# Sliding-window attention in front of an MLP: 64 queries against 128 keys in six of eight batches, instead of 128 keys against 192 queries

## The chip, the cores and the metric

The kernel runs on one core of one Trainium2 chip, in one launch. The metric is the device time in microseconds (us) of that core; less is better. The time before is the median of 13 runs, 317.54 us, and single runs lie between 315.99 and 318.42 us.

## The reference, cut to what matters

Causal attention in which a query sees itself and the 63 keys before it, then a two-layer MLP with a hard-swish on the 4608 rows that the attention gives. All inputs are float32.

```python
B, H, S, D = 8, 8, 576, 64;  window = 64
scores = q @ k.transpose(0, 1, 3, 2) / sqrt(D)
rel = pos[:, None] - pos[None, :]            # query minus key
mask = (rel >= 0) & (rel < window)
attn = softmax(where(mask, scores, -1e9))
x = (attn @ v).transpose(0, 2, 1, 3).reshape(B * S, H * D)      # 4608 x 512
h = x @ w_in                                                     # 512 x 2048
out = (h * clip(h + 3, 0, 6) / 6) @ w_out                        # 2048 x 512
```

## The kernel before

The attention of a batch is cut into four groups `g` of two heads (NG = 4), the MLP into nine blocks `T` of 512 rows (TB = 512). The weights, cast to bf16, stay in SBUF. Every matmul is bf16.

**Order of the work.** The program is written for a planner (`Plan`): Python code walks through TensorE's work in order and keeps a clock of its own; the other engines' instructions go into a heap with a ready time, an estimated duration and dependencies, and are written down in the order in which the planner's clock reaches them. What comes out is one fixed instruction order for each engine. On the chip an instruction waits only for semaphores; a queue is never reordered.

**The main loop** runs over T. `s1(T)` is the first MLP layer: 8 chunks of 8 matmuls of 512 columns (L661), ScalarE's relu (L670) and VectorE's product (L673) into `gT`. It needs `xT`, the transposed attention output. `s2(T)` is the second layer: 4 row tiles of 16 matmuls (L705), each result copied by ScalarE (L722) and stored (L725). Into `s2(T)` the attention of batch b = T + 1 is woven at fixed places, for b from 2 on by `REST`:

```python
REST = ((4, "S", 0), (10, "S", 1), (16, "S", 2), (17, "PV", 0), (22, "S", 3), (23, "PV", 1),
        (29, "PV", 2), (36, "PV", 3))
```

The number says how many of the 64 matmuls of L705 are issued before. So a score unit `S` and a product unit `PV` stand between two L705 matmuls, and TensorE does nothing else while it waits in one.

**S** (`scores`) puts keys on partitions: five blocks of 128 keys, each against the 192 queries that can see them (64 for the last), for both heads. K = 64 is half of the array's rows, so head 0 uses the upper and head 1 the lower half: 10 matmuls (L552). ScalarE takes the exponential out of PSUM (L561, L567), VectorE multiplies by a 0/1 band mask (L572, 1920 elements).

**PV** (`pv`) multiplies the block pT (keys on partitions, 128 queries) by V with a column of ones appended (VW = 65 columns): each of the five query blocks needs the key block of its own and the one before, so 18 matmuls for both heads (L589, L594), accumulated in PSUM. VectorE divides by the ones column (L604, L607) and a DMA transposes the result into `xT` (L614).

**Loads.** From batch 2 on, q, k and v come in by DMA in five pieces each (four of 128 rows, a tail `tl` of 64), are cast to bf16 by GpSimd (L262), and q and k are then transposed by two large DMAs (L393) into `QKT`. V is cast straight into `V_ring`, rows of keys on partitions, five casts a batch. All DMAs are issued by SyncE's queue in the planner's order; a load of piece n waits in the program for the DMA eight before it. `load_v` (from L328), `load_nat` (from L386) and `load_items` set the order: q, k, v of a batch, with the stores and transposes in between.

Batches 0 and 1 (b < NR6) go another way, with transposes on TensorE (L521, 64x64 tiles of the array in pairs), and aren't touched by the change.

Of the kernel before, what the change touches and what calls it, by code (L numbers as in the profile page):

```python
# [10 lines left out]
F32 = mybir.dt.float32  # L11
BF16 = mybir.dt.bfloat16
EXP = mybir.ActivationFunctionType.Exp
# [8 lines left out]
NQT = 1  # L22
# [79 lines left out]
def kernel(  # L102
# [69 lines left out]
    neg = consts.tile([P, TB], BF16, name="neg")  # L172
    half = consts.tile([P, 1], F32, name="half")
    mask32 = consts.tile([P, QW], F32, name="mask32")
    mask = consts.tile([P, 2 * KB, QW], BF16, name="mask")
    win16 = consts.tile([P, NG, FF], BF16, name="win16")
    wout16 = consts.tile([P, NFC, DM], BF16, name="wout16")
    xT = consts.tile([P, NG, XR * S + P - D], BF16, name="xT")
    gT = consts.tile([P, NFC, TB], BF16, name="gT")
    runs = [[consts.tile([P, R, D], BF16, name=f"run{i}{j}") for j in range(NR6 * NG)] for i in range(2)]  # L180
    natural = [consts.tile([P, NG, KB, P], BF16, name=f"nat{i}") for i in range(2)]
    QK_tiles = [consts.tile([P, 2 * NG, SP], BF16, name=f"QKT{i}") for i in range(NQT)]

# [3 lines left out]

    P_ring = [consts.tile([P, 2, KB, 2 * P], BF16, name=f"pT{i}") for i in range(NPT)]
    V_ring = [consts.tile([P, NG, KB, 2, VW], BF16, name=f"V{i}") for i in range(2)]

    nc.vector.memset(idle[:], 0.0)
    make_identity(nc, ident32)
# [16 lines left out]
    def band(t, fill):  # L209
# [118 lines left out]
    def load_v(b):  # L328

        V = V_ring[b % 2]  # L330
        tiles = {}
        deps = stage_slot([("cast", b, 2, i) for i in range(KB - 1)])
        if b >= 2:
            deps += (("pv", b - 2, NG - 1),)
        if b == 2:
            deps += (("issued", b, 1),)
        if b > 2:
            deps += (("s1v", b - 1),)
        tdeps = tail_slot([("cast", b, 2, KB - 1)])
        for kb in range(KB):  # L340
            ss = min(P, S - kb * P)
            def go(s, kb=kb, ss=ss):
                if kb == 0:
                    tiles["t"] = stage.tile([P, 4, H * D], F32, name="st", tag="st")
                if kb == KB - 1:
                    st = tails.tile([P, H * D], F32, name="tl", tag="tl")[:ss, :]
                else:
                    st = tiles["t"][:, kb, :]
                nc.sync.dma_start(  # L349
                    out=st.rearrange("p (h d) -> p h d", h=H),  # L350
                    in_=v[b, :, kb * P : kb * P + ss, :].rearrange("h s d -> s h d"),
                )
# [153 lines left out]
    def soft(b, g):  # L506
        return [("mask", b, g)] if b else [("exp", b, g, i) for i in range(2)]

    def vcasts(b, g):
        return [("cast", b, 2, g // 2, kb) for kb in range(KB)] if b == 0 else [("cast", b, 2, kb) for kb in range(KB)]  # L510
# [66 lines left out]
                  msk if part and not add else None)  # L577
        pl.mark(("S", b, g), pl.t)

    def pv(b, g):  # L580
        for r in soft(b, g) + vcasts(b, g):
            pl.wait(r)
        V = V_ring[b % 2]
        pT = P_ring[(b * NG + g) % NPT]
        o = two_banks([("op", b, g)])
        for h in range(2):
            for qb in range(KB):
                ob = o[:, h, qb * VW : (qb + 1) * VW]
                nc.tensor.matmul(  # L589
                    ob, lhsT=pT[:, h, qb, 0:P], rhs=V[:, g, qb, h, :],  # L590
                    start=True, stop=(qb == 0),
                )
# [5 lines left out]
        pl.pe(0.55)  # L598
        pl.mark(("pv", b, g), pl.t)
        ov = o[:, :, 0 : KB * VW].rearrange("p h (k w) -> p h k w", w=VW)  # L600
        cell = {}
        def norm(s):
            rec = small.tile([P, 2, KB], F32, name="rec", tag="rec")
            nc.vector.reciprocal(out=rec[:].unsqueeze(3), in_=ov[:, :, :, D:VW])  # L604
            opg = opool.tile([P, KB, 2, D], BF16, name="opg", tag="opg")
            cell["o"] = opg
            nc.vector.tensor_tensor(  # L607
                out=opg[:].rearrange("p k h d -> p h k d"), in0=ov[:, :, :, 0:D],
                in1=rec[:].unsqueeze(3).to_broadcast([P, 2, KB, D]), op=MULT,
            )  # L610
        def xdma(t):
            def fn(s):
                x0 = x_at(b)
                nc.sync.dma_start_transpose(  # L614
                    out=xT[:, g, x0 : x0 + SP].rearrange("d (k t) -> d k t", t=P),
                    in_=cell["o"][:].rearrange("p k h d -> p (k h d)"),
                )
# [125 lines left out]
    def unit(f, b, g):  # L743
        if f == "T":
            tqk(b, g)
        elif f[0] == "S":
            scores(b, g, (0, 1) if f == "S" else (int(f[1]),))
# [59 lines left out]
```

## Time and profile before

| what | value |
|---|---|
| median of 13 runs | 317.54 us (315.99 to 318.42) |
| profiled execution: its own time | 318.25 us |
| profiled execution: span, first to last instruction | 316.5 us |
| granted TensorE clock, mean | 0.992 |
| busy, of the span | PE 305.1 us (96%), DVE 172.1 (54%), ACT 165.6 (52%), POOL 92.0 (29%) |
| DMA | 58.34 MB, mean 184 GB/s |
| L705 / L661 matmuls | 136.6 us busy x576 / 126.6 us busy x704 |
| L552 (S) / L589 and L594 (PV) | 18.4 us busy x320 / 22.0 x320 and 21.0 x256 |
| L262 V casts of 128 rows / of the tail | 605 ns mean x30 / 1246 ns mean x8 |
| L572 mask | 1252 ns mean x28 |

PE is TensorE, PEld its weight loads, DVE is VectorE, ACT is ScalarE, POOL is GpSimd, SP is SyncE; "SPq" rows are DMA issues by SP's queue. The profiled execution is 1.7 us longer than its span. Matmuls overlap in their pipeline, so a row's length says less than the distance between the starts of two rows. A bracket at a timeline row holds the engine's idle time before it and what ended it.

### The profile page before, as it was taken

How to read it: one execution, taken by the hardware profiler on the slowest of the kernel's cores; microseconds unless marked ns; L12 is line 12 of the kernel's file. 1: busy time of each engine (PE TensorE's matmuls, PEld its weight loads, DVE VectorE, ACT ScalarE, POOL GpSimd, SP SyncE). 2: the span in 40 equal slices, each digit the busy share in tenths (PEclk: the TensorE clock that was granted, in tenths of full speed). 3: DMA queues.
4: the chain of work that ended last, by engine and by line, in shares of the span. 5: the costliest groups of instructions: out<-in, count | busy, mean ns of one | idle time of the engine just before them, and what ended most of it. 6: DMA issues, size and time to landing. Idle time of an engine off the chain costs nothing.

```text
span 316.5 us, 6169 instructions
## 1 busy us (share of the span) xinstructions
PE 305.1 (96%) x2531; PEld 158.3 (50%) x2531; DVE 172.1 (54%) x204; ACT 165.6 (52%) x218; POOL 92.0 (29%) x132
## 2 busy tenths in 40 slices
PE   6989997999999999999999999999999999999995
PEld 2554344644554455775544454445575544444442
DVE  5486646847833684377526761777167716404700
ACT  5755536566715691469236833682368336316511
POOL 3157747412640265016501660066003000000000
PEclk9799999999999999999999999999999999999999
DMA  7899999999999999999999999999993630010011
GB/s 226 220 322 390 387 332 220 237 177 215 204 211 188 223 207 215 157 244 195 217 164 223 206 207 173 241 199 217 198 214 59 120 91 0 33 68 33 0 68 66
DMA packets 153340, 58.34 MB, mean 184 GB/s; under 512 B 142048, under 2 KB 143072, under 8 KB 153312
## 3 DMA queue, kind: packets, MB, share of 16 engines
q1 hardware_dynamic: 153312, 57.95, 83.8%
q8 instruction: 20, 0.33, 0.4%
q14 instruction: 8, 0.07, 0.1%
HBM read 36.70 MB, written 9.44 MB: 146 GB/s over the span
## 4 chain that ended last, share of the span: by engine, by line
PE 70%; DMA 15%; SPq 9%; DVE 2%; POOL 1%; issue 1%; ACT 0%; ACTq 0%
PE acc L705 32%; PE ps L661 31%; DMA st<-in_moe_w_out_dram 4%; DMA st<-in_k_dram 3%; DMA st<-in_moe_w_in_dram 3%; PE ps L552 3%; PE ps L589 2%; SPq L318 2%; SPq L349 2%; PE ps L594 2%; SPq L393 2%; DMA tl<-in_v_dram 2%; DMA st<-in_q_dram 1%; SPq L373 1%; DMA xT<-opg 1%; DVE opg L607 1%
## 5 line engine op out<-in xcount | busy, mean ns | idle before, releaser
L673 DVE SCALAR_TENSOR_TENSOR gT<-t,ps 128x1024 bf16<-128x1024 bf16 x72 | 87.9, 1221 | 98.6 <-ACT t L670 98.6
L705 PE MATMUL acc<-wout,gT 128*128 128x512 bf16 x576 | 136.6, 380 | 1.5 <-POOL wout L262 1.1
L661 PE MATMUL ps<-xT,win 128*128 128x512 bf16 (+4 forms) x704 | 126.6, 341 | 0.1
L670 ACT ACTIVATE t<-ps,half 128x1024 bf16<-128x1024 f32 x72 | 80.2, 1113 | 50.5 <-PE ps L661 50.5
L661 PEld LDWEIGHTS <-win 128*128 128x128 bf16 x704 | 65.2, 98 | 60.3 <-issue 1.0
L705 PEld LDWEIGHTS <-gT 128*128 128x128 bf16 x576 | 52.9, 98 | 59.4 <-issue 1.7
L722 ACT COPY osb<-acc 128x512 f32<-128x512 f32 x36 | 21.1, 589 | 73.1 <-PE acc L705 62.8
L561 ACT ACTIVATE pT<-ps 128x768 bf16<-128x768 f32 x64 | 48.9, 811 | 8.7 <-PE ps L552 8.4
L262 POOL CAST V<-st 128x512 bf16<-128x512 f32 (+1 forms) x30 | 18.1, 605 | 108.8 <-DMA st<-in_v_dram 92.9
L262 POOL CAST nat<-st 128x512 bf16<-128x512 f32 x48 | 34.4, 725 | 15.6 <-DMA st<-in_k_dram 8.5
L572 DVE TENSOR_TENSOR pT<-pT,mask 128x1920 bf16<-128x1920 bf16 x28 | 35.1, 1252 | 6.8 <-ACT pT L567 6.8
L607 DVE TENSOR_TENSOR opg<-ps,rec 128x640 bf16<-128x640 f32 x32 | 26.4, 825 | 1.1
L589 PEld LDWEIGHTS <-pT 128*128 128x128 bf16 x320 | 20.6, 97 | 6.1 <-ACT pT L561 0.7
L589 PE MATMUL ps<-V,pT 128*128 128x65 bf16 x320 | 22.0, 194 | 1.1 <-POOL V L262 0.6
L594 PE MATMUL ps<-V,pT 128*128 128x65 bf16 x256 | 21.0, 193 | 0.0
L552 PEld LDWEIGHTS <-QKT 64*128 64x128 bf16 x320 | 11.1, 95 | 16.3 <-issue 15.1
L552 PE MATMUL ps<-QKT 64*128 64x192 bf16 (+1 forms) x320 | 18.4, 237 | 0.1
L594 PEld LDWEIGHTS <-pT 128*128 128x128 bf16 x256 | 17.9, 98 | 0.7 <-issue 0.7
L259 DVE CAST run<-st 128x576 bf16<-128x576 f32 x15 | 7.6, 512 | 10.9 <-DMA st<-in_q_dram 7.2
L262 POOL CAST V<-tl 64x512 bf16<-64x512 f32 (+1 forms) x8 | 10.0, 1246 | 10.8 <-DMA tl<-in_v_dram 10.7
L261 ACT COPY QKT<-ps 128x1152 bf16<-128x1152 bf16 x6 | 6.7, 1124 | 11.0 <-PE ps L521 10.9
L604 DVE RECIPROCAL rec<-ps 128x10 f32<-128x10 f32 x32 | 6.9, 215 | 6.6 <-PE ps L594 6.5
(45 smaller groups left out, 87.4 us busy)
## 6 DMA issues: line engine op xcount, KB each, us to landing
out_dram<-osb SPq DMA_DIRECT2D x36, 256.0 KB, 2.7
st<-in_v_dram SPq DMA_DIRECT2D x28, 256.0 KB, 5.3
st<-in_q_dram SPq DMA_DIRECT2D x24, 256.0 KB, 5.5
st<-in_k_dram SPq DMA_DIRECT2D x24, 256.0 KB, 5.2
st<-in_moe_w_out_dram SPq DMA_DIRECT2D x4, 1024.0 KB, 14.7
st<-in_moe_w_in_dram SPq DMA_DIRECT2D x3, 1024.0 KB, 10.6
st<-in_q_dram SPq DMA_DIRECT2D x8, 288.0 KB, 6.1
st<-in_k_dram SPq DMA_DIRECT2D x8, 288.0 KB, 6.8
```

The costliest lines, as they stand in the source:

```text
L262: return lambda s: nc.gpsimd.tensor_copy(out=out_ap, in_=in_ap) and None
L552: nc.tensor.matmul(st[:, h, off : off + w], lhsT=KT[h * D : (h + 1) * D, kb * P : (kb + 1) * P], rhs=QT[h * D : (h + 1) * D, kb * P : kb * ...
L561: nc.scalar.activation(out=pT[:, :, kbs[0] : kbs[0] + 2, 0:QW], in_=st[:, :, 0 : 2 * QW].rearrange("p h (k w) -> p h k w", k=2), func=EXP, ...
L572: pl.op("DVE", t, 1.2, lambda s: nc.vector.tensor_tensor(out=pT[:, :, :, 0:QW], in0=pT[:, :, :, 0:QW], in1=mask[:].rearrange("p (h k) w -> ...
L589: nc.tensor.matmul(ob, lhsT=pT[:, h, qb, 0:P], rhs=V[:, g, qb, h, :], start=True, stop=(qb == 0),)
L594: nc.tensor.matmul(ob, lhsT=pT[:, h, qb - 1, P : 2 * P], rhs=V[:, g, qb - 1, h, :], start=False, stop=True,)
L607: nc.vector.tensor_tensor(out=opg[:].rearrange("p k h d -> p h k d"), in0=ov[:, :, :, 0:D], in1=rec[:].unsqueeze(3).to_broadcast([P, 2, KB ...
L661: nc.tensor.matmul(hT[:, j, dst : dst + w], lhsT=win16[:, g, (2 * c + j) * P : (2 * c + j + 1) * P], rhs=xT[:, g, src : src + w], start=(g ...
L670: nc.scalar.activation(out=t1[:], in_=hT[:], func=RELU, bias=half[:], scale=1.0 / 6.0)
L673: nc.vector.scalar_tensor_tensor(out=gT[:, 2 * c : 2 * c + 2, :], in0=cell["t"][:], scalar=1.0, in1=hT[:], op0=MIN, op1=MULT,)
L705: nc.tensor.matmul(accs[ts], lhsT=gT[:, fc, ts * P : (ts + 1) * P], rhs=wout16[:, fc, :], start=(fc == 0), stop=(fc == NFC - 1),)
L722: nc.scalar.copy(out=osb[:], in_=acc)
```

## The change

For batches 2 to 7 the unit of attention becomes a block of 64 queries. Its window reaches exactly over the 128 keys that end with it, so each of the nine blocks needs one score matmul and one PV matmul for each head.

- `scores64` replaces `scores`: 18 matmuls of 64 columns, 128 keys as weights, the heads again on the two row halves of the array. ScalarE reads 640 and 512 elements instead of 768, 768 and 128; the mask is one operation on 1152 elements, with a 64-wide mask `mask64` that is repeated.
- `pv64` replaces the old PV (kept as `pv128` for batches 0 and 1): 20 matmuls of 65 columns with 64 queries as weights and nothing accumulated. An even block's output goes to partitions 0 to 63, an odd one's to 64 to 127, so the two use different halves of the array's columns. The ninth block is computed twice to fill the last pair.
- An odd block's keys are one 128-key piece of V. An even block's keys straddle two pieces, so V is held a second time, shifted by 64 rows, in `W_ring`. It lies in the memory of the `run` tiles, which batches 0 and 1 no longer need by then. GpSimd makes it: for each of four pieces of V there are three casts (64 rows into W, 128 rows into V, 64 rows into W) where there was one; for the tail one, as before.
- Memsets for W and a small setup of `mask64` are added on GpSimd and VectorE. The planner's durations of S and PV are changed.

```diff
-    runs = [[consts.tile([P, R, D], BF16, name=f"run{i}{j}") for j in range(NR6 * NG)] for i in range(2)]
+    runs_all = consts.tile([P, 2, NR6 * NG, R, D], BF16, name="runs")
+    runs = [[runs_all[:, i, j] for j in range(NR6 * NG)] for i in range(2)]
...
+    W_ring = [runs_flat[:, i * NV : (i + 1) * NV].rearrange("p (g k h w) -> p g k h w", g=NG, k=KB, h=2) for i in range(2)]
+    mask64 = consts.tile([P, D], BF16, name="mask64")
...
+    at("POOL", 17.2, 0.2, lambda: nc.gpsimd.memset(m64[:], 1.0))
+    at("POOL", 17.3, 0.3, lambda: nc.gpsimd.affine_select(
+        out=m64[:], in_=m64[:], pattern=[[1, D]], compare_op=ISGE, fill=0.0, base=D, channel_multiplier=-1))
+    at("POOL", 17.4, 0.3, lambda: nc.gpsimd.affine_select(
+        out=m64[:], in_=m64[:], pattern=[[-1, D]], compare_op=ISGE, fill=0.0, base=-1, channel_multiplier=1), "m64")
+    pl.op("DVE", 26.2, 0.1, lambda s: nc.vector.tensor_copy(out=mask64[:], in_=m64[:]) and None, "mask64", deps=("m64",))
+    for i, t in enumerate(W_ring):
+        pl.op("POOL", 0.0, 0.3, lambda s, t=t: nc.gpsimd.memset(t[:, :, :, :, D:VW], 1.0) and None, ("w1", i), deps=(("T", NR6 - 1, NG - 1),))
+        pl.op("POOL", 0.0, 0.6, lambda s, t=t: nc.gpsimd.memset(t[0:D, :, 0, :, :], 0.0) and None, ("w0", i), deps=(("w1", i),))
...
-                casts(("cast", b, 2, kb), land, [(
-                    ("POOL",), V[:ss, :, kb, :, 0:D], st.rearrange("p (g h d) -> p g h d", g=NG, h=2), H * D)])
+                sv = st.rearrange("p (g h d) -> p g h d", g=NG, h=2)
+                if b < NR6:
+                    todo = [(("POOL",), V[:ss, :, kb, :, 0:D], sv, H * D)]
+                else:
+                    W = W_ring[b % 2]
+                    todo = [(("POOL",), W[D:P, :, kb, :, 0:D], sv[0:D], H * D)]
+                    if ss == P:
+                        todo.append((("POOL",), V[:, :, kb, :, 0:D], sv, H * D))
+                        todo.append((("POOL",), W[0:D, :, kb + 1, :, 0:D], sv[D:P], H * D))
+                casts(("cast", b, 2, kb), land, todo)
...
+    def kwin(b, g, i, h):
+        t = QK_tiles[b % NQT]
+        c = (2 * g + 1 if b < NR6 else NG + g) * SP + (i - 1) * D
+        return t[:].rearrange("p a s -> p (a s)")[h * D : (h + 1) * D, c : c + P]
...
+    def scores64(b, g):
...
+        for part in range(2):
+            i0, i1 = ((0, 5), (5, BL))[part]
+            st = two_banks([("exp", b, g, part)])
+            for i in range(i0, i1):
+                for h in range(2):
+                    c = (i - i0) * D
+                    nc.tensor.matmul(
+                        st[:, h, c : c + D], lhsT=kwin(b, g, i, h), rhs=QT[h * D : (h + 1) * D, i * D : (i + 1) * D],
+                        start=True, stop=True,
+                    )
...
+    def pv64(b, g, o):
+        V, W, pT = V_ring[b % 2], W_ring[b % 2], blocks(b, g)
+        for h in range(2):
+            for m in range(KB):
+                for odd in range(2):
+                    i = min(2 * m + odd, BL - 1)
+                    nc.tensor.matmul(
+                        o[odd * D : (odd + 1) * D, h, m * VW : (m + 1) * VW],
+                        lhsT=pT[:, h, i * D : (i + 1) * D],
+                        rhs=(V if i % 2 else W)[:, g, m, h, :], start=True, stop=True,
+                    )
+        pl.pe(0.5)
```

In the built program the places of S and PV in the L705 stream stay as `REST` has them. On SP's queue a store moves before the last two k loads of batch 2, and from batch 2 on the third `xT` transpose of a batch is issued before a store instead of after it.

More of the change, by code (lines that the diff above doesn't have):

```diff
@@ L174 @@
     mask32 = consts.tile([P, QW], F32, name="mask32")
+    m64 = consts.tile([P, D], F32, name="m64")
     mask = consts.tile([P, 2 * KB, QW], BF16, name="mask")
@@ L189 @@
     V_ring = [consts.tile([P, NG, KB, 2, VW], BF16, name=f"V{i}") for i in range(2)]
+    runs_flat = runs_all[:].rearrange("p a b c d -> p (a b c d)")
+    NV = NG * KB * 2 * VW
+    W_ring = [runs_flat[:, i * NV : (i + 1) * NV].rearrange("p (g k h w) -> p g k h w", g=NG, k=KB, h=2) for i in range(2)]
+    BL = S // D
+    mask64 = consts.tile([P, D], BF16, name="mask64")
     nc.vector.memset(idle[:], 0.0)
@@ L578, in scores, with blocks, ex, msk @@
         pl.mark(("S", b, g), pl.t)
-    def pv(b, g):
-        for r in soft(b, g) + vcasts(b, g):
-            pl.wait(r)
+    def kwin(b, g, i, h):
+        t = QK_tiles[b % NQT]
+        c = (2 * g + 1 if b < NR6 else NG + g) * SP + (i - 1) * D
+        return t[:].rearrange("p a s -> p (a s)")[h * D : (h + 1) * D, c : c + P]
+    def blocks(b, g):
+        n = b * NG + g
+        return P_ring[n % NPT][:].rearrange("p h k w -> p (h k w)")[:, 0 : 2 * S].rearrange("p (h c) -> p h c", h=2)
+    def scores64(b, g):
+        for i in range(2):
+            pl.wait(("tr", b, i))
+        QT, pT = qk(b, 0, g), blocks(b, g)
+        for part in range(2):
[8 more added lines that the diff above has]
+                    )
+            pl.pe((0.25, 0.22)[part])
+            def ex(s, st=st, i0=i0, i1=i1):
+                nc.scalar.activation(
+                    out=pT[:, :, i0 * D : i1 * D], in_=st[:, :, 0 : (i1 - i0) * D], func=EXP, scale=scale,
+                )
+            def msk(t):
+                pl.op("DVE", t, 0.8, lambda s: nc.vector.tensor_tensor(
+                    out=pT.rearrange("p h (i w) -> p (h i) w", w=D), in0=pT.rearrange("p h (i w) -> p (h i) w", w=D),
+                    in1=mask64[:].unsqueeze(1).to_broadcast([P, 2 * BL, D]), op=MULT,
+                ) and None, ("mask", b, g), deps=("mask64",))
+            pl.op("ACT", pl.t + 0.1, (0.8, 0.69)[part], ex, ("exp", b, g, part), msk if part else None)
+        pl.mark(("S", b, g), pl.t)
@@ new lines, in pv64 @@
+    def pv64(b, g, o):
[8 more added lines that the diff above has]
+                        rhs=(V if i % 2 else W)[:, g, m, h, :], start=True, stop=True,
+                    )
+        pl.pe(0.5)
@@ L583, in pv, with pv128 @@
+    def pv128(b, g, o):
         V = V_ring[b % 2]
         pT = P_ring[(b * NG + g) % NPT]
-        o = two_banks([("op", b, g)])
         for h in range(2):
@@ L598, in pv @@
         pl.pe(0.55)
+    def pv(b, g):
+        for r in soft(b, g) + vcasts(b, g):
+            pl.wait(r)
+        o = two_banks([("op", b, g)])
+        if b >= NR6:
+            pl.need(("w0", b % 2))
+            pv64(b, g, o)
+        else:
+            pv128(b, g, o)
         pl.mark(("pv", b, g), pl.t)
@@ L746, in unit @@
         elif f[0] == "S":
-            scores(b, g, (0, 1) if f == "S" else (int(f[1]),))
+            if b < NR6:
+                scores(b, g, (0, 1) if f == "S" else (int(f[1]),))
+            else:
+                scores64(b, g)
         elif f == "PV":
```

## The prediction

> **What bounds the kernel now.** I read the page's engine totals first.
>
> ```profile
> PE 305.1 (96%) x2531; PEld 158.3 (50%) x2531; DVE 172.1 (54%) x204; ACT 165.6 (52%) x218; POOL 92.0 (29%) x132
> PEclk9799999999999999999999999999999999999999
> DMA  7899999999999999999999999999993630010011
> ```
>
> TensorE is busy 96% of the span, at full clock from the third slice on, but so are the DMA engines, up to slice 30 of 40 (some 240 us). So a second view, the timeline of SP's queue over one batch: it issues without a pause, and the next batch's first V load comes 32.05 us after the last one's (167.89, 199.94), while TensorE's own step, from PV of one batch to PV of the next, is 32.1 to 32.6 us. The two run abreast.
>
> ```profile
> 167.89 0.57 SPq L349 DMA_DIRECT2D st<-in_v_dram  x1
> ...
> 185.37 0.57 SPq L725 DMA_DIRECT2D out_dram<-osb  x1
> 186.05 2.61 SPq L614 DMA_TRANSPOSE xT<-opg  x2
> 189.11 0.36 SPq L725 DMA_DIRECT2D out_dram<-osb  x1
> 189.57 2.55 SPq L614 DMA_TRANSPOSE xT<-opg  x2
> 192.21 0.53 SPq L725 DMA_DIRECT2D out_dram<-osb  x1
> 192.84 7.04 SPq L393 DMA_TRANSPOSE QKT<-nat  x2
> 199.94 0.58 SPq L349 DMA_DIRECT2D st<-in_v_dram  x1
> ```
>
> Third, TensorE's timeline, where the distance between starts is the price: L521 in batch 1, then S in batch 5.
>
> ```profile
> 46.90 0.76 PE L521 MATMUL ps<-ident,run 64*64 64x64 bf16 x36
> 47.59 0.82 PE L705 MATMUL acc<-wout,gT 128*128 128x512 bf16 x3
> ```
>
> ```profile
> 174.45 1.03 PE L705 MATMUL acc<-wout,gT 128*128 128x512 bf16 x4
> ...
> 175.41 0.53 PE L552 MATMUL ps<-QKT 64*128 64x192 bf16 x10
> ...
> 175.88 1.47 PE L705 MATMUL acc<-wout,gT 128*128 128x512 bf16 x6
> ...
> 177.28 0.53 PE L552 MATMUL ps<-QKT 64*128 64x192 bf16 x10
> ```
>
> L705 runs at 0.216 us (28 of them take 6.04 in the chain that ended last). Four from 174.45 end at 175.31, S begins at 175.41: 0.10 lost on entering the half-array form. S to S is 1.87, less six L705 makes **0.57 for one S unit**. A PV unit, in the full-array form, has no such loss: L705 x6 at 182.83 gives way to the next PV at 184.13 and resumes at 184.68, **0.55**, or 0.031 for each of 18 matmuls with a weight load each.
>
> Last, GpSimd's V casts and the PV that needs them, and the mask.
>
> ```profile
> 173.93 0.62 POOL L262 CAST V<-st 128x512 bf16<-128x512 f32 x1 [1.89 <-DMA st<-in_v_dram]
> ...
> 175.13 0.62 POOL L262 CAST V<-st 128x512 bf16<-128x512 f32 x1 [0.58 <-DMA st<-in_v_dram]
> ...
> 176.62 0.62 POOL L262 CAST V<-st 128x512 bf16<-128x512 f32 x1 [0.88 <-DMA st<-in_v_dram]
> ...
> 177.50 1.16 DVE L572 TENSOR_TENSOR pT<-pT,mask 128x1920 bf16<-128x1920 bf16 x1 [0.48 <-ACT pT L567]
> ...
> 177.69 1.46 POOL L262 CAST V<-tl 64x512 bf16<-64x512 f32 x1 [0.45 <-DMA tl<-in_v_dram]
> ...
> 179.84 0.23 PE L589 MATMUL ps<-V,pT 128*128 128x65 bf16 x2
> ```
>
> V is ready at 179.15, 0.69 before its PV. The tail cast, begun inside the mask, takes 1.46 where an equal one elsewhere takes 0.61: it ends 0.49 after the mask, so a GpSimd cast seems to stand still while this VectorE operation runs.
>
> **The change, part by part.** *S on TensorE, 24 units.* Price of a pair of 64-column matmuls, x, and of leaving the half-array form, e: L521 gives 18x + e = 0.69; old S, with four pairs of 192 columns at 0.081 (0.216 x 192/512) and one of 64, gives 0.47 = 0.324 + x + e. So x = 0.032, e = 0.114. New S: 0.10 + 9 x 0.032 + 0.114 = 0.50, saving 0.07. Bounds: 0.29 if entry and exit cost nothing, 0.79 if the halves took turns; L552's pairs start together, so I take 0.50.
>
> *PV on TensorE, 24 units.* No row shows two column tiles with the same 128 rows. If they run side by side like L521's pairs: 0.10 + 10 x 0.032 + 0.114 = 0.53, saving 0.02, for the form change is now paid here too. If they take turns: 20 x 0.031 + 0.214 = 0.83, costing 0.28. Without a form change: 0.32, saving 0.23. I take 0.53: L521 is nearest, it loads 64-column weights on 64-column tiles and keeps a pair at 0.032.
>
> A rule of the Trainium skill speaks against this. "TensorE: Matmul & The Clock Gate", Part 3, The mechanism, says that a weight load overlaps a running matmul only where the row groups differ, which two column tiles never do; its LDWEIGHTS section gives columns/1.2 ns, an estimated 53 ns for 64 columns, so by these pages alone a PV would be near 20 x (53 + 27) ns = 1.6 us and the kernel some 25 us slower. The trace's L589 and L594 rows, all on one row group, follow each other every 0.031 with a load each, so the rule does not hold there as it stands; whether it holds for column tiles no row shows.
>
> So TensorE saves 4 x 0.09 = 0.36 us a batch, 2.2 in all.
>
> *V casts on GpSimd.* Eight more for each batch, 4.96 us at 0.62. In the built program the second and third cast of a piece each wait for the cast before; the gap at such a wait is 0.07 to 0.08 (L210 ends at 18.78, L214 starts at 18.86). Piece to piece overlaps by 0.05. So a piece costs 3 x 0.62 + 2 x 0.07 - 0.05 = 1.95, and pieces land 1.2 to 1.5 apart: GpSimd falls behind. Batch 5, from its second piece: 173.93 + 3 x 1.95 + 0.62 = 180.40. The masks come earlier and shrink to some 0.75 (1.16 x 1152/1920 = 0.70, and fixed cost); two of them fall into this stretch, each stopping a cast for 0 to 0.75. I take 0.75 together: V ready at 181.15, when PV would start at 179.84 - 3 x 0.07 = 179.63. **TensorE waits**, and behind that PV stand the remaining L705, S3 and all later work. The casts that move 64 rows to other partitions have no row; an unblocked 64-row cast takes 0.61. Bounds: 0.55 (three casts in 1.72 at 185.60) to 0.9, between it and the blocked 1.46; I take 0.62.
>
> *It is not paid six times.* SP's queue never waits for TensorE in these rows, so V lands when it did, and TensorE, once late, finds the next V readier. V ready against the old PV start, with first casts and PV starts read likewise in each batch 2 to 7: +2.6, +1.7, +1.2, +1.3, +1.2, +0.7. Each batch wins 0.36 back, and waits of 0.20 and 0.43 for `xT` at the next s1 (96.6 and near 161) vanish. Lateness at PV: 2.6; 2.6 - 0.36 - 0.20 = 2.1; 1.7; 1.7 - 0.36 - 0.43 = 0.9, but V says 1.3; 1.2; 0.8. After the last PV start an S and four PV save 0.15: **+0.7**.
>
> *DMA.* Bytes stay. A store issued before batch 2's last k loads can push the loads by its 0.57; I add half, 0.3. The third `xT` transpose ahead of a store needs a result that is ready 3 us before, so nothing queued behind it on SP waits.
>
> *Hidden.* ScalarE's exponentials lose some 0.6 a unit (1152 elements in two operations instead of 1664 in three, at 0.81 for 768), and masks 0.4: no S or PV waits for either now. Setup of `mask64` on GpSimd, 0.9, sits in its 2.13 idle before the weight cast at 21.33, and costs 0.9 without that. W's memsets, 2.0, come before V's tail of batch 1; seven more L705 (1.5) move in front of that PV, and the wait at batch 2 swallows what is left.
>
> **Sum.** 0.7 + 0.3 = +1.0 on the profiled execution's 318.25, which lies 0.71 above the median of 317.54: a median of 318.5. A measurement of this kernel can tell 0.2%, 0.63 us, from no change.
>
> **Rivals.** *Column tiles take turns.* PV at 0.83: TensorE's step grows by 4 x (0.28 - 0.07) = 0.84 a batch, it falls behind all DMAs, and the lateness runs 2.6, 3.2, 4.1, 4.5, 5.3, 6.2, with the last PVs +7.2: 324.7. Then the change does not do what it says. For it: no row of such tiles. Against: L521. 20%.
>
> *Moving V across partitions costs more.* W casts at 0.9: a piece is 2.51, V(7) ready at 237.74 + 7.53 + 0.62 + 0.75 = 246.6, 2.4 late: 319.4 to 322. For it: 1.17 for a 128x576 cast at 49.48. 11%.
>
> *The other side: casts keep up.* At 0.55 with no mask in the way, batch 5's ten casts take 5.5 from 173.93 and V is there at 179.5, before 179.63. It decides when a cast costs under 0.57. Then TensorE's 0.36 counts until it runs into `xT`: that of batch 6 is issued last at 222.85 and lands 2.8 later, some 0.8 before TensorE needs it, so the end is at most 0.8 + 0.36 early: 316.4 to 317.5. For it: GpSimd is 29% busy; against: the waits between casts. 17%.
>
> My forecast has 52%, 317.5 (no mask in the way) to 319.4 (each stops a cast whole).
>
> **How the numbers follow.** Time 318.5. Range 317.0 to 324.8: below lie some 10%, above 9%. Faster: 10% of the keep-up case. Same: its other 7% and 15% of the forecast. Slower: 37 + 20 + 11 = 68%.
>
> **What would show it.** PV units starting behind a GpSimd V cast in batches 2 and 5; S to S at 1.80 instead of 1.87; a PV at 0.53 with starts in pairs 0.03 apart; V tail casts 2 us later; SP's rows unchanged to 240 us. A PV near 0.83, pauses in SP's rows, or `xT` waits at every s1 would prove me wrong.

## The result, and the profile after

The changed kernel takes 321.5 us (median; single runs 318.39 to 324.48). The kernel before, run beside it, takes 317.14 us. The ratio is 1.0118, with a 95% interval of 1.0096 to 1.0139: the change makes the kernel **1.2% slower**. The ratio leaves out two slow runs of the eleven (323.76 and 324.48, over 1.5% above the fastest), so it stands for some +3.7 us, while the two medians differ by 4.4. Its profiled execution is 319.52 us long, with a span of 317.7 us, 1.2 us above before's span. That profiled execution lies near the fast end of the runs, so it alone does not explain the median.

The page's totals and its chain of waits, of the changed kernel:

```profile
PE 302.1 (95%) x2771; PEld 152.7 (48%) x2771; DVE 165.4 (52%) x205; ACT 154.2 (49%) x194; POOL 122.7 (39%) x187
...
PE 53%; DMA 16%; POOL 12%; SPq 11%; issue 3%; DVE 1%; ACT 1%; POOLq 0%; ACTq 0%
```

TensorE is busy 3.0 us less than before (305.1), GpSimd 30.7 us more (92.0). In the chain that ended last, GpSimd now has 12% of the span, where it had 1%. Next, three groups of TensorE (after the bar: busy time, mean ns of one; after the second bar: idle time just before, and what ended it):

```profile
L745 PE MATMUL ps<-xT,win 128*128 128x512 bf16 (+4 forms) x704 | 126.4, 341 | 1.2 <-DMA xT<-opg 1.1
L650 PE MATMUL ps<-runs,pT 128*64 128x65 bf16 x288 | 13.1, 198 | 3.2 <-POOL runs L279 3.2
L626 PE MATMUL ps<-QKT 64*128 64x64 bf16 x432 | 10.5, 191 | 0.0
```

The new PV (L650, with W shown under the name `runs` whose memory it uses) waits 3.2 us for GpSimd's casts. S (L626) waits for nothing. s1 (L745, L661 before) waits for `xT`.

The units themselves cost what was forecast. In TensorE's timeline, S of batch 5:

```profile
173.84 0.44 PE L626 MATMUL ps<-QKT 64*128 64x64 bf16 x18
174.21 1.47 PE L789 MATMUL acc<-wout,gT 128*128 128x512 bf16 x6
175.61 0.44 PE L626 MATMUL ps<-QKT 64*128 64x64 bf16 x18
```

S to S is 1.77; less six L789 (L705 before, 0.216 each) that is 0.47 for one S, where the same reading gave 0.57 before. Four microseconds after the first of these rows the first PV of this batch meets the casts (rows of PE, GpSimd and VectorE from the whole timeline):

```profile
176.03 1.02 POOL L279 CAST V<-st 128x512 bf16<-128x512 f32 x1
...
177.11 0.62 POOL L279 CAST runs<-st 64x512 bf16<-64x512 f32 x1
177.20 1.14 DVE L636 TENSOR_TENSOR pT<-pT,mask 128x1152 bf16<-128x1152 bf16 x1 [0.62 <-ACT pT L632]
...
177.79 1.02 POOL L279 CAST runs<-tl 64x512 bf16<-64x512 f32 x1
...
178.12 0.20 PE L650 MATMUL ps<-runs,pT 128*64 128x65 bf16 x1
178.13 0.20 PE L650 MATMUL ps<-V,pT 128*64 128x65 bf16 x1
...
178.87 0.23 PE L650 MATMUL ps<-runs,pT 128*64 128x65 bf16 x3 [0.48 <-POOL runs L279]
```

The reader is to see three things. A pair of column tiles starts together (178.12 and 178.13), so the two halves run side by side. PV does not wait at its start: head 0 walks through all pieces of V, and stops where the piece is not cast yet, at the last even block, until the tail's cast ends at 178.81. And a cast that meets a mask can take 1.02 instead of 0.62, while this mask takes 1.14.

**A ledger for all runs.** T = 0, which the change does not touch, ends at another time in each execution: s1 of T = 1 begins between 60.6 and 63.1 us, and latest in before's own profile (63.10; after 62.05). So I compare the stretch from the first s1 matmul of T = 1 to the first s2 matmul of T = 8. S and PV units are measured as the extra distance between the neighbouring L705-type matmuls. The 48 units of batches 2 to 7 take 27.25 us before (0.5 of it waits in S), and 24.09 when nothing is late (the last kernel below). So TensorE saves 3.16 us. Stretch and waits of a row come from the kernel's one profiled execution, the ratio from its timed runs, so the two need not agree: late_pv's profile is the shortest of its five runs.

| kernel | ratio to before, 95% interval | stretch, us | against before's 235.54 | waits in first PVs for V, us | waits for `xT` at s1, us |
|---|---|---|---|---|---|
| after | 1.0118 (1.0096 to 1.0139) | 237.89 | +2.35 | 4.4 | 1.5 |
| again | 1.0162 (1.0106 to 1.0219) | 241.45 | +5.91 | 5.2, and 4.1 at half clock | 0.1 |
| no_w | 1.0031 (1.0002 to 1.0060) | 236.05 | +0.51 | 0 | 4.1 |
| w_unread | 1.0235 (1.0180 to 1.0291) | 243.97 | +8.43 | 7.3, and 3.4 us at half clock | 0 |
| late_pv | 1.0067 (1.0029 to 1.0106) | 235.35 | -0.19 | 1.6 | 1.8 |
| fill_wait | 1.0158 (1.0096 to 1.0221) | 239.61 | +4.07 | 7.6 with the filling | 0 |
| w_act | 1.0553 (1.0499 to 1.0608) | 252.73 | +17.19 | 0 (16.0 in S) | 0 |
| no_w_half_st | 0.9918 (0.9884 to 0.9952) | 234.03 | -1.51 | 0.3 | 1.8 |
| before_half_st | 0.9985 (0.9956 to 1.0013) | 234.90 | -0.64 | 0 | 0 |
| v_early | 1.0033 (1.0001 to 1.0065) | 236.61 | +1.07 | 1.4 | 3.3 |
| before_v_early | 1.0010 (0.9987 to 1.0033) | 234.82 | -0.72 | 0 | 0.3 |
| v_early_defer | 0.9935 (0.9911 to 0.9958) | 233.62 | -1.92 | 0 | 1.6 |
| before_defer | 0.9965 (0.9941 to 0.9989) | 234.90 | -0.64 | 0 | 0 |

A row can be added up: after is -3.16 (units) + 4.4 (V) + 0.9 (`xT`: 1.5 against 0.6 before) = +2.1, and 2.35 was measured. v_early is -3.16 + 1.4 + 2.7 = +0.9, measured 1.07.

### The profile page after: what moved, and what is told of

Its sections match the earlier page's. It is cut to its first block, busy times and chain, and to the rows that moved or that the text cites. A ratio compares the mean times of both kernels' runs of the same rounds, so it can differ in the third digit from the quotient of the medians.

```text
span 317.7 us, 6648 instructions
## 1 busy us (share of the span) xinstructions
PE 302.1 (95%) x2771; PEld 152.7 (48%) x2771; DVE 165.4 (52%) x205; ACT 154.2 (49%) x194; POOL 122.7 (39%) x187
## 3 DMA queue, kind: packets, MB, share of 16 engines
q1 hardware_dynamic: 153312, 57.95, 85.2%
## 4 chain that ended last, share of the span: by engine, by line
PE 53%; DMA 16%; POOL 12%; SPq 11%; issue 3%; DVE 1%; ACT 1%; POOLq 0%; ACTq 0%
PE acc L789 28%; PE ps L745 21%; POOL runs L279 8%; SPq L418 5%; DMA st<-in_v_dram 5%; DMA st<-in_moe_w_out_dram 4%; POOL V L279 4%; DMA st<-in_k_dram 4%; PE ps L650 3%; DMA st<-in_moe_w_in_dram 3%; SPq L698 2%; SPq L398 2%; SPq L335 2%; PE ps L626 1%; SPq L809 1%
## 5 line engine op out<-in xcount | busy, mean ns | idle before, releaser
L789 PE MATMUL acc<-wout,gT 128*128 128x512 bf16 x576 | 136.7, 380 | 1.4 <-POOL wout L279 1.0
L745 PE MATMUL ps<-xT,win 128*128 128x512 bf16 (+4 forms) x704 | 126.4, 341 | 1.2 <-DMA xT<-opg 1.1
L754 ACT ACTIVATE t<-ps,half 128x1024 bf16<-128x1024 f32 x72 | 80.1, 1113 | 51.8 <-PE ps L745 51.8
L745 PEld LDWEIGHTS <-win 128*128 128x128 bf16 x704 | 65.1, 98 | 60.9 <-issue 1.7
L789 PEld LDWEIGHTS <-gT 128*128 128x128 bf16 x576 | 52.6, 98 | 59.0 <-issue 1.5
L279 POOL CAST runs<-st 64x512 bf16<-64x512 f32 (+1 forms) x49 | 32.8, 670 | 82.7 <-DMA st<-in_v_dram 80.0
L632 ACT ACTIVATE pT<-ps 128x640 bf16<-128x640 f32 (+1 forms) x48 | 28.7, 650 | 13.3 <-PE ps L626 13.2
L636 DVE TENSOR_TENSOR pT<-pT,mask 128x1152 bf16<-128x1152 bf16 x24 | 21.9, 912 | 4.7 <-ACT pT L632 4.7
L650 PE MATMUL ps<-runs,pT 128*64 128x65 bf16 x288 | 13.1, 198 | 3.2 <-POOL runs L279 3.2
L650 PEld LDWEIGHTS <-pT 128*64 128x64 bf16 x480 | 10.1, 111 | 11.6 <-issue 5.9
L586 ACT ACTIVATE pT<-ps 128x768 bf16<-128x768 f32 x16 | 12.6, 818 | 3.2 <-PE ps L577 3.1
L276 DVE CAST runs<-st 128x576 bf16<-128x576 f32 x15 | 7.6, 512 | 9.5 <-DMA st<-in_q_dram 6.8
L626 PEld LDWEIGHTS <-QKT 64*128 64x128 bf16 x432 | 7.6, 95 | 10.2 <-issue 10.2
L650 PE MATMUL ps<-V,pT 128*64 128x65 bf16 x192 | 12.2, 199 | 0.1
L278 ACT COPY QKT<-ps 128x1152 bf16<-128x1152 bf16 x6 | 6.8, 1127 | 10.5 <-PE ps L546 10.5
L626 PE MATMUL ps<-QKT 64*128 64x64 bf16 x432 | 10.5, 191 | 0.0
```

Of the source, the lines that this page charges most:

```text
L279: return lambda s: nc.gpsimd.tensor_copy(out=out_ap, in_=in_ap) and None
L626: nc.tensor.matmul(st[:, h, c : c + D], lhsT=kwin(b, g, i, h), rhs=QT[h * D : (h + 1) * D, i * D : (i + 1) * D], start=True, stop=True,)
L632: nc.scalar.activation(out=pT[:, :, i0 * D : i1 * D], in_=st[:, :, 0 : (i1 - i0) * D], func=EXP, scale=scale,)
L636: pl.op("DVE", t, 0.8, lambda s: nc.vector.tensor_tensor(out=pT.rearrange("p h (i w) -> p (h i) w", w=D), in0=pT.rearrange("p h (i w) -> p ...
L650: nc.tensor.matmul(o[odd * D : (odd + 1) * D, h, m * VW : (m + 1) * VW], lhsT=pT[:, h, i * D : (i + 1) * D], rhs=(V if i % 2 else W)[:, g, ...
L745: nc.tensor.matmul(hT[:, j, dst : dst + w], lhsT=win16[:, g, (2 * c + j) * P : (2 * c + j + 1) * P], rhs=xT[:, g, src : src + w], start=(g ...
```

## The experiments

Theory A: GpSimd's eight extra casts a batch hold the first PV. Theory B: the changed order of SP's queue and of the transfers does it.

**again**: the changed kernel as it is, run a second time.

> The changed kernel once more. Both theories: 1.0 to 1.4% above the kernel before in the timed rounds. Its profiled execution was 1.27 us over the one of before, the median of its runs some 4 us, so a second profile may show where a slower execution spends the rest. Theory A (V's eight extra GpSimd casts hold the first PV of a batch): the waits at those six PV units, 4.4 us in the first profile, are larger in a slower execution. Theory B (SP's queue, reordered, lets data land later): TensorE waits for xT at the start of s1, 1.5 us in the first profile, grow instead.

Measured 322.31 us, 1.0162. Its profiled execution is a long one (322.42), and shows the part that the first profile lacks. As theory A expected, the waits for V are larger (5.2 us for 4.4); the waits for `xT`, which theory B expected to grow, fall to 0.1. TensorE's timeline in batch 2:

```profile
80.31 0.19 PE L650 MATMUL ps<-runs,pT 128*64 128x65 bf16 x1
...
81.74 0.19 PE L650 MATMUL ps<-runs,pT 128*64 128x65 bf16 x1 [1.23 <-POOL runs L279]
82.42 0.19 PE L650 MATMUL ps<-V,pT 128*64 128x65 bf16 x1 [0.49 <-POOL V L279]
83.77 0.27 PE L650 MATMUL ps<-runs,pT 128*64 128x65 bf16 x3 [1.17 <-POOL runs L279]
...
84.65 1.91 PE L789 MATMUL acc<-wout,gT 128*128 128x512 bf16 x4 [0.33 <-issue]
86.50 0.66 PE L626 MATMUL ps<-QKT 64*128 64x64 bf16 x18
```

and the windows of the same time (after the busy times of PE, PEld, DVE, ACT and POOL come the granted clock, the DMA share and GB/s):

```profile
76.00:80.00 4.00, 3.95 (x67) 2.05 (x67) 3.03 (x3) 3.10 (x6) 3.63 (x7) 1.00 1.33 197
80.00:84.00 4.00, 1.12 (x18) 0.64 (x19) 0.53 (x1) 1.32 (x3) 3.69 (x6) 0.89 1.34 199
84.00:88.00 4.00, 3.67 (x48) 1.75 (x47) 1.73 (x3) 1.01 (x2) 4.00 (x7) 0.50 1.26 209
```

The first PV stops three times, each time released by a cast, for 3.4 us in all by the starts of its matmuls. Then **the granted clock is 0.5** for 6.8 us from 83.1. The stretch from the end of the waits to PV2 of the batch is 2.7 us longer than in after's profile. The same happens in batch 6: 1.8 us of waits, then 3.4 us at 0.5 from 216.2, 1.4 us lost. So the row adds up to -3.16 + 5.2 + 4.1 - 0.5 = +5.6, measured 5.91. Why batch 2's wait is longer here: T = 0 was done 0.8 us earlier (61.23 against 62.05), but the first piece of V landed 1.4 us later (74.02 against 72.61). An early TensorE meets a late V.

**no_w**: the eight extra casts of a batch are left out (W keeps old contents).

```diff
-                    todo = [(("POOL",), W[D:P, :, kb, :, 0:D], sv[0:D], H * D)]
-                    if ss == P:
-                        todo.append((("POOL",), V[:, :, kb, :, 0:D], sv, H * D))
-                        todo.append((("POOL",), W[0:D, :, kb + 1, :, 0:D], sv[D:P], H * D))
+                    todo = [(("POOL",), V[:, :, kb, :, 0:D], sv, H * D)]
+                    if ss < P:
+                        todo = [(("POOL",), W[D:P, :, kb, :, 0:D], sv[0:D], H * D)]
```

> The eight extra casts per batch are left out (W keeps old contents except for the tail, so even query blocks meet wrong values); TensorE's work, the masks and SP's order are those of the changed kernel. Theory A: no TensorE wait at PV, and TensorE's gain of some 0.45 us a batch (S 0.464 for 0.561, PV 0.54 for 0.556) counts until xT limits it: 0.2 to 0.8% faster than before, 314.5 to 316.5 us. Theory B: SP's order is unchanged, so it stays 0.8 to 1.2% slower than before.

Measured 317.67 us, 1.0031: the loss is nearly gone, with SP's order as in after. Theory A holds, B falls as the main cause. But TensorE's saving does not show either, and A's 314.5 to 316.5 is missed. TensorE's timeline at s1 of T = 5:

```profile
189.65 0.71 PE L744 MATMUL ps<-xT,win 128*128 128x512 bf16 x2
191.84 1.02 PE L744 MATMUL ps<-xT,win 128*128 128x512 bf16 x4 [1.48 <-DMA xT<-opg]
193.49 0.81 PE L744 MATMUL ps<-xT,win 128*128 128x512 bf16 x3 [0.62 <-DMA xT<-opg]
```

TensorE gets there earlier and waits for `xT`, 4.1 us in all s1: the gain has turned into a new wait.

**w_unread**: the other half alone. The old S and PV, with the extra casts made and not read. They are nine a batch, one more than in the change, since the tail is cast into V too.

```diff
+                    else:
+                        todo.append((("POOL",), V[:ss, :, kb, :, 0:D], sv, H * D))
...
-            pv64(b, g, o)
-        else:
-            pv128(b, g, o)
+        pv128(b, g, o)
...
-            if b < NR6:
-                scores(b, g, (0, 1) if f == "S" else (int(f[1]),))
-            else:
-                scores64(b, g)
+            scores(b, g, (0, 1) if f == "S" else (int(f[1]),))
```

> The kernel before with the eight extra casts per batch (and the tail cast twice, so nine), W never read: TensorE's work of before, GpSimd's work of the change and one cast more. Theory A: TensorE waits at the first PV of a batch as in the change, without its gain: 1.2 to 2.0% slower than before, 321 to 323.5 us. Theory B: only the store ahead of the k loads of batch 2 is left of SP's reordering: within 0.5% of before.

Measured 324.4 us, 1.0235. The first PVs of the six batches take 4.6, 2.5, 0.6, 0.6, 1.9 and 0.6 us instead of 0.56, and the clock is 0.5 for 3.4 us from 85.2. The casts without the new units cost more than the whole change. What the ninth cast and the old, longer masks have in this was not tried alone.

**late_pv**: PV units later in s2.

```diff
-    REST = ((4, "S", 0), (10, "S", 1), (16, "S", 2), (17, "PV", 0), (22, "S", 3), (23, "PV", 1),
-            (29, "PV", 2), (36, "PV", 3))
+    REST = ((4, "S", 0), (10, "S", 1), (16, "S", 2), (27, "PV", 0), (28, "S", 3), (32, "PV", 1),
+            (36, "PV", 2), (40, "PV", 3))
```

> The change with the PV units placed later in the stream of the second layer (27, 32, 36, 40 instead of 17, 23, 29, 36; S3 at 28): the first PV comes 2.16 us later, with other matmuls in front of it. Theory A: the waits at PV fall from 4.4 us to under 1; what is left is xT, whose last transposes come 0.9 us later: 0.3 to 1.0% faster than the change, about the kernel before (316.5 to 319). Theory B: V is no matter, xT comes later still: the same as the change or slower.

Measured 319.19 us, 1.0067. The first PVs still wait 1.6 us together (batches 2 and 7, 0.8 each), more than the 1 us forecast, and s1 waits 1.8 us for `xT`, which is now made later. By the ratios some half of the loss is gone, which supports theory A.

**fill_wait**: does the clock fall because TensorE stands still?

```diff
+        fill = two_banks([]) if g == 0 and b in (2, 6) else None
         for h in range(2):
             for m in range(KB):
+                if fill is not None and h == 0:
+                    for _ in range(2):
+                        nc.tensor.matmul(fill[:, 0, :], lhsT=idle[:, 0:P], rhs=idle[:], start=True, stop=True)
```

> The changed kernel with two added matmuls of 512 columns (on a tile of zeros, result unread, 0.43 us a pair) in front of each of the five pairs of head 0 in the first PV of batches 2 and 6, 2.16 us a unit, so that TensorE has work while it waits for pieces of V. Clock theory (a long, scattered wait for V brings the granted clock down to 0.5 for 3.4 to 6.8 us, and that makes the median of the changed kernel 2 us longer than its undisturbed profile): no 0.5 stretch in the trace, mean clock 0.995 or more, median 319.5 to 320.5, nearer to the profiled 319.5 than to 322. Wait theory (the wait itself is longer in the slower executions, the clock follows from nothing): 322 or more, since the added work does nothing for V. In the profile the first PV of batches 2 and 6 should take about 2.7 to 3.0 from its start, and if V is later than that no more than V's delay.

Measured 322.26 us, as again. The clock stayed at 1.000 in three of four executions and 0.995 in one (in again 0.979, 0.988, 0.989, 0.995). So the clock did stay up, but the time is no better, and the clock theory's number is missed. The filling was too dear: the two units take some 4.35 us each, since the filled pairs stand 0.69 apart for 0.43 of added matmuls, and the added tile had to wait for an exponential:

```profile
81.11 0.59 PE L651 MATMUL ps<-idle 128*128 128x512 bf16 x2 [0.59 <-ACT pT L632]
```

The run is consistent with the idle time bringing the clock down, and leaves the clock's price in the median unmeasured.

**w_act**: everything computed, W's eight casts on ScalarE.

```diff
-                    todo = [(("POOL",), W[D:P, :, kb, :, 0:D], sv[0:D], H * D)]
+                    todo = [(("ACT",) if ss == P else ("POOL",), W[D:P, :, kb, :, 0:D], sv[0:D], H * D)]
...
-                        todo.append((("POOL",), W[0:D, :, kb + 1, :, 0:D], sv[D:P], H * D))
+                        todo.append((("ACT",), W[0:D, :, kb + 1, :, 0:D], sv[D:P], H * D))
```

> The whole changed kernel, but the eight extra casts of a batch into W are made by ScalarE; GpSimd casts V once a piece as before. Theory A (the GpSimd casts hold the first PV): the waits for V in the first PV of batches 2 to 7 fall from 4.4 us in all to under 1.5, no clock stretch at 0.5, and the time is that of the run without W casts, 317 to 318.5, so about level with the kernel before. Rival (ScalarE, in order, now stands waiting for pieces of V that have not landed, and its relu, exponentials and copies of results queue behind: about 6 casts of 0.6 and their waits per batch): 320 or more, with TensorE waiting for ScalarE at L705 or at s1 and not for GpSimd.

Measured 334.64 us, 1.0553. PV waits for no cast any more, so A's first half holds, but its time is 16 us off, and the clock is 0.5 for 6.8 us from 80.1. The rival's number is right and its reason is mostly not: in the whole run ScalarE's casts wait 1.6 us for V. They stand between the relus of s1. ScalarE's timeline:

```profile
183.19 1.11 ACT L754 ACTIVATE t<-ps,half 128x1024 bf16<-128x1024 f32 x1
184.32 1.27 ACT L278 CAST runs<-st 64x512 bf16<-64x512 f32 x2
185.62 1.11 ACT L754 ACTIVATE t<-ps,half 128x1024 bf16<-128x1024 f32 x1
```

A chunk of s1 takes TensorE 1.73 us, and ScalarE now 2.4 (185.62 - 183.19) where two casts follow a relu. An engine that is busy 49% of the span has, in this stage, only 0.6 us to spare for each chunk. TensorE loses the time in S, behind the late relus, as its waits show (in all, times, longest):

```profile
PE ps L626 <- DVE gT L757: 9.3, 11, 1.0
PE ps L626 <- ACT pT L632: 6.7, 6, 5.2
```

**no_w_half_st and before_half_st**: is it the transfers that take TensorE's gain? In both, in T = 1 to 7, every second store of a result tile is dropped; the first has no extra casts either.

```diff
-            pl.op("SP", t, 0.1, fn, ("st", nst))
+            if 1 <= T < NTB - 1 and ts % 2:
+                pl.mark(("st", nst), t)
+            else:
+                pl.op("SP", t, 0.1, fn, ("st", nst))
```

> The changed kernel without the eight extra casts and, in T = 1 to 7, without every second store of a result tile (14 stores of 262 KB, 3.7 MB of 58.3, left out). DMA theory (TensorE's 2.2 to 2.6 us are saved but are lost again at s1, where xT arrives no earlier, because the transfers are the bound): the xT waits at s1 vanish and the time is 314.3 to 315.5, 1.5 to 2.5 below the kernel before with the same stores left out. Rival (the gain is lost elsewhere: in more exits from half-array forms, in PSUM or in ScalarE): 316.5 or more, level with the control.

> Control: the kernel before without the same 14 stores. If TensorE's work alone bounds it, 316.5 to 317.2 (the 0.6 us of waits for xT that its trace shows go away); if the transfers bound it too, 315 or less, since 3.7 MB at 184 GB/s are 20 us of transfers.

Measured 314.37 us (0.9918) and 316.61 us (0.9985). With 3.7 MB less to move, the faster units are worth 2.2 us; with all of it, they are worth nothing (no_w). The kernel before hardly gains, since it hardly waits for transfers. So the transfers, not another TensorE cost, take the gain. Two things stay open: a dropped store frees its bytes and also its half microsecond on SP's queue, and the runs do not separate the two; and the waits for `xT` were to vanish, but no_w_half_st's profile, an execution 2 us above the median, still has 1.8 us of them.

**v_early and before_v_early**: two of V's five pieces are loaded ahead of the QKT transposes.

```diff
+        soon = deps + ((("op", b - 1, 1) if b > 2 else ("issued", b, 0),) if b >= 2 else ())
...
-            yield b, deps + tdeps if kb == KB - 1 else deps, go
+            yield b, soon if kb < 2 else deps + tdeps if kb == KB - 1 else deps, go
```

> The whole changed kernel with its casts as they are, but the first two pieces of V of a batch are loaded earlier: for batches 3 to 7 behind the first xT transpose of the batch before (where the trace of the changed kernel shows transfer engines at 0.48 of busy and 89 GB/s for 4 us) instead of behind the two QKT transposes, for batch 2 between its two QKT transposes. Theory (V's three casts a piece are late only because all pieces land in the last 10 us, and the transfers are late because the queue has a hole while it waits for PV): six casts are done before the other pieces land, what is left behind the last pieces is some 2 x 1.95 + 0.62 = 4.5 us, so V is ready 2.5 us earlier, the waits for V in the first PV of batches 2 to 7 fall from 4.4 us in all to under 0.8, and the saved 2.2 us of TensorE show at least in part: 314.5 to 317, at least level with the kernel before and 4 us or more below the changed one. Rival (the early pieces only push the xT transposes and QKT back, as the transfers are the bound): waits for xT or for QKT of 0.5 and more at each s1 or S0, 318 to 321.

> Control: the kernel before with the same two pieces of V loaded earlier. Its TensorE is bound by its own work but for 0.6 us of waits, so by both theories 316 to 317.5, no more than 1 us below the kernel before; if loads in the hole are worth something by themselves, 315 or less.

Measured 318.18 us (1.0033) and 317.27 us (1.0010). The place for them is seen in windows of after's profile and of v_early's (the last two columns are the DMA share and GB/s); first after:

```profile
188.00:192.00 4.00, 4.00 (x19) 1.76 (x18) 0.00 (x0) 0.89 (x2) 0.00 (x0) 1.00 0.48 89
```

then v_early:

```profile
188.00:192.00 4.00, 4.00 (x20) 1.83 (x19) 0.00 (x0) 0.63 (x2) 2.93 (x5) 1.00 1.28 143
```

In after, the transfer engines are at less than half and GpSimd is idle (0.00), while SP's queue issues nothing but `xT` transposes and stores; in v_early both work there. It is the deepest hole of its kind; in the 4 us from 89, 123 and 154 of after's profile, by the earlier `xT` transposes, the share is 0.73 to 0.78. The waits for V fall from 4.4 to 1.4 us, all of them in batch 2: the casts are as many and as long as in after, only earlier, and most of the change's loss is gone (318.18 against 322.31 in again). But `xT` waits rise to 3.3 us, 2.4 of them at the s1 from 94.0, so neither forecast is met in full: the V part was right, the transfers took the rest, and 318.18 lies between the two.

**v_early_defer and before_defer**: nothing left out; seven of the 36 stores are issued after the first store of T = 7, when the loads are over. They are held in free memory. The first run has v_early's loads too, the control has not.

```diff
...
-            osb = osbp.tile([P, DM], F32, name="osb", tag="osb")
+            osb = HOLD[T, ts]() if (T, ts) in HOLD else osbp.tile([P, DM], F32, name="osb", tag="osb")
...
-            pl.op("SP", t, 0.1, fn, ("st", nst))
+            if (T, ts) in HOLD:
+                pl.mark(("st", nst), t)
+                late.append(fn)
+            else:
+                pl.op("SP", t, 0.1, fn, ("st", nst))
+                if T == NTB - 2:
+                    while late:
+                        pl.op("SP", t, 0.1, late.pop(0))
```

> The run with two early pieces of V, and besides seven of the 36 stores (T = 0: 2, T = 1: 2, T = 2, 3, 4: 1 each; 1.8 MB) held back in free SBUF (the rest of the run tiles behind W, the unused ends of the pT tiles, one new tile) and issued after the first store of T = 7, when the transfer engines have little to do. Nothing is left out. Transfer theory (TensorE's saving of 2.2 us is lost at s1, since the transfers of a batch take as long as TensorE's step): the waits for xT, 3.3 us in the run before (2.4 of them at the s1 from 94.0), fall under 0.8, no wait for V over 0.3 is left, and the time is 314 to 315.5, about 0.7% below the kernel before. Rival (the stores do not stand in the way, the queue's order around xT does): 317 or more, with the waits for xT as they were.

> Control: the kernel before with the same seven stores held back, in the memory of the run tiles. Its TensorE hardly waits for transfers (0.6 us of xT waits), and it gained 0.15% when 14 stores were left out, so by both theories 316.3 to 317.3, level with the kernel before or up to 0.3% below.

Measured **314.93 us**, 0.9935 (0.9911 to 0.9958), and 315.73 us, 0.9965 (0.9941 to 0.9989). The first is the only complete version with the new units that beats the kernel before. TensorE's groups in it:

```profile
L755 PE MATMUL ps<-xT,win 128*128 128x512 bf16 (+4 forms) x704 | 126.6, 340 | 1.2 <-DMA xT<-opg 1.2
L660 PE MATMUL ps<-runs,pT 128*64 128x65 bf16 x288 | 12.2, 197 | 0.0
```

No PV waits for a cast any more, and the clock is 0.998 to 1.000 in all 12 executions. The control says what this is worth: holding stores back gives the old units 1.4 us, more than was forecast, and the new units 0.8 us on top of that, a difference at the edge of what these runs resolve. The old units with both the early loads and the held stores were not run; the early loads alone gave them nothing (before_v_early). 1.6 us of waits for `xT` are left.

## Why the prediction was right or wrong

The direction was right (slower), and so was its mechanism: the first PV of a batch waits for GpSimd's extra casts (no_w, w_unread). The size was wrong: +1.0 us was forecast, and the median rose by 4.4 (321.5 - 317.14; 3.7 by the ratio). That the time lies inside the range is luck: the upper bound of 324.8 was there for the column tiles that take turns, which did not come. It lies outside the forecast's own 317.5 to 319.4, and in the bracket of the rival with dearer casts without that rival's mechanism, for an unblocked cast to other partitions took the 0.62 that was taken. In the terms of the sum, after's profile has -3.2 us in the units where -2.2 was forecast, 4.4 us of waits for V where the listed latenesses amount to some 3.5 (2.8 at batch 2, 0.4 at batch 5, 0.3 at batch 6), and +0.9 for `xT` where -0.6 was forecast; the rest of the median's rise lies in longer executions than this one.

- **S unit, 0.50.** Measured 0.464. Pairs follow each other every 0.030, close to the 0.032 taken; leaving the form costs a little less than forecast.
- **PV unit, 0.53 if the column tiles run side by side.** Measured 0.534 to 0.546 where nothing is late. The rival with tiles that take turns (0.83) is out. The Trainium skill's rule on weight loads that the prediction weighed ("TensorE: Matmul & The Clock Gate", Part 3, The mechanism) does not hold for these tiles either: the pairs follow each other every 0.03 us with two loads each.
- **TensorE saves 2.2 us.** Measured 3.16: 2.7 from the units, and half a microsecond of waits in S that the new kernel no longer has.
- **A piece of V costs 1.95 of GpSimd.** Measured 3 x 0.68 = 2.04 when no mask is in the way, since a gap of 0.06 stands before the next piece too. A mask adds 0.4 or more to most casts that run beside it alone (11 of 17 in after's profile), and takes 0.91 on average instead of the 0.75 estimated.
- **V lands when it did.** This assumption failed. SP's queue does follow TensorE: V's loads stand behind the QKT transposes, these behind `xT`, and that behind PV, for whose results (`rec` and `opg` of VectorE) the queue waits at `xT` 10.5 us in all before, and 15.0 after. In after's profile the fourth `xT` transpose ahead of batch 5 is issued at 156.40 instead of 159.26, and V's first load at 165.41 instead of 167.89. TensorE's s2 there begins at 172.88 instead of 174.45. So V moved with TensorE, and further; how much of it is the tie and how much the changed order of the queue is not shown. The tail cast of batch 5 ends at 178.81, no later than before's 179.15, where 2 us later was forecast, and SP's rows, which were to stay, moved. The waits did not fade from batch to batch.
- **"It is not paid six times"**, with a lateness of 2.6 us at batch 2 that sinks to 0.8. This is the step that failed. The waits per batch are 1.19, 0, 0.56, 0.67, 1.65 and 0.34 in after's profile, and 3.4 and 1.8 in batches 2 and 6 of again. That they come back fits a V that is tied to TensorE. They differ from execution to execution; in batch 2 the wait was longer where T = 0 ended earlier (again), but two profiles do not show a rule. (The prediction's 2.1 for batch 3 is 2.04 by its own terms, which changes nothing.)
- **Each batch wins 0.36 back, and the waits for `xT` vanish.** The first is true of TensorE alone. The waits for `xT` grew, from 0.6 to 1.5 us, and to 4.1 without the casts; they vanish only where TensorE is held up more (0.1 in again). That the two "run abreast" was read from the profile, but what follows from it, that a faster TensorE only waits, was counted in the keep-up rival alone.
- **The clock.** No term of the sum had it. In again the half clock cost 4.1 us.
- **The base.** The sum was made against a profiled execution whose T = 0 ended late (63.10). In the stretch that the change touches, after's profile is +2.35, not the +1.2 that the two spans show.
- **Hidden work** (shorter exponentials, masks, setup) stayed hidden: L626 waits for nothing. A cost of the store ahead of batch 2's k loads (+0.3) was not tried alone.

What stays open is how the median's +4.4 divides between longer waits and the slow clock, since only one of the changed kernel's long executions has a profile. The granted clock on record sets a bound: it is 0.988 to 0.995 in the eleven timed executions of the changed kernel and 1.000 in the profiled one. One minus the clock, times the span, is 1.6 to 3.8 us, 2.8 on average, so by this estimate the slow clock costs at most that; in the kernel before, beside the experiments, the same product is 0.2 to 0.5 on average.

## What to carry to other kernels

Work that is moved onto an engine with much of its time free is paid where that engine's results are due, so count its queue from the moment the data lands to the moment the consumer starts, in that stage. A gain on the busiest engine counts only up to the next resource that runs abreast of it: find the slack of the transfers before the gain is booked, and look in windows for a stretch where their share drops, because that hole is where loads can go. And compare two profiles over the stretch that the change touches, for what lies before it can differ by more than the change.

## What the runs showed of the hardware

- Matmuls of 64 weight columns on the two column halves, with the same 128 rows, start mostly 3 to 4 ns apart, and pairs follow each other every 0.03 us with a weight load each.
- A GpSimd cast and a VectorE bf16 product of two operands that run at the same time can stretch each other: 0.62 becomes 1.02, and 0.75 becomes 1.14. Not every meeting does it: 6 of the 17 casts in after's profile that run beside a mask alone keep their 0.62.
- The granted clock fell to 0.5 after 1.8 us of waits inside one PV (again, batch 6: the longest single stop was 1.4 us from start to start), and stayed there for 3.4 us; after's profile has 1.65 us of waits at the same place, and w_unread one stop of 2.0 us (118.19 to 120.21), and no fall. In w_act one stop of 5.4 us (76.40 to 81.77) brought 6.8 us at 0.5. The Trainium skill, "TensorE: Matmul & The Clock Gate", Part 1, HAM oscillation, puts the danger at idle gaps above some 3.4 us. The slow stretches of these runs are 3.4 or 6.8 us long, once or twice that figure, and the runs show that scattered stops well below it can be enough, though they need not be.
